# Two chunks of query projections moved from the projection phase into the first segment of the attention

## The chip, the cores and the metric

The kernel runs on one core of one Trainium2 chip. The metric is the device time of one execution in microseconds; the time before is the median of three runs. Tables and quotations from the profile come from one profiled execution of the same kernel.

## The reference: what is computed

Two attention branches work on the same input `x` (2048 positions, width 512, 32 heads of 16):

```
A:  q,k,v = x @ wqkv;  p = softmax(q k^T / 4) over all 2048 keys;  a = (p v) @ wo
B:  q,k,v = x @ wq, wk, wv;  4 segments of 512: causal softmax inside a segment,
    plus a memory of earlier segments (phi(q) M / phi(q) z), mixed by sigmoid(beta);  b = (...) @ wo
out = g a + (1 - g) b,   g = sigmoid(sum(x * gate_w))
```

Only branch A's queries are touched here: `q = x @ wqkv[:, 0:512]`, for 2048 positions in four chunks of 512.

## The kernel before, in words

All products that need full precision are made of two halves: a float32 tile is split into a rounded part (`h`) and its remainder (`l`), and three matmuls, h·l, l·h and h·h, stand for one.

**Projections (lines 277 to 588).** A chunk of 512 positions of `xT` is loaded, split and multiplied. `qk_tile` (line 358) makes one tile: 128 output columns (8 heads, ordered by dimension) by 512 positions, in 4 x 3 = 12 matmuls of 128x512 on line 313. One tile fills one *slot* (`slot`, line 306); other work is posted to a slot and one of four places in it. ScalarE copies the tile out (lines 368, 369), VectorE makes its remainder (line 376), and SP's queue stores both parts in DRAM scratch (`qd`, `kd`; lines 370, 377). Phase A (lines 472 to 484) takes each of the four chunks through 4 tiles of Q, 4 of K and 4 of V: 12 slots a chunk. The next chunk's load and split, and at the last chunk those of branch B's weights, are posted by slot numbers counted from `s0`, the chunk's first slot. Phase B (lines 552 to 587) does the same for branch B, and runs the first 96 maxima of the attention beside it.

**Attention (lines 591 to 985).** A *unit* is a side (A or B), a group of four heads and one segment of 512 queries: `(side, g, c)`. Units stand in the order A0 B0 A1 B1 ... of segment 1 (c = 0), then segment 2, and so on; each A unit has 64 slots, each B unit 10 (592 slots a segment, 2368 in all). A slot is one 128x512 tile of scores. The main loop (line 944) goes through the slots n in an order written out by hand, engine by engine:

- `score_part` (line 662): TensorE makes a score tile (`st`, line 677), ScalarE exponentiates it (line 700). For B, GpSimd masks the diagonal (line 681).
- `max_part` (line 218), 96 slots ahead: TensorE makes the same scores the other way round (`sm`, line 204) in one of four PSUM banks, and VectorE reduces them to maxima (`TENSOR_REDUCE`, line 225; for B a masked minimum, line 237). The maxima become extra rows of the query tile, so that the exponentials of line 700 need no further subtraction.
- every third slot a turn of TensorE: either `some_values` (line 712), which multiplies finished exponentials with V into the bank `ops` (line 733), or, if the list `shared` holds anything, four matmuls of that list in its place.
- when a unit's values are complete, ScalarE copies `ops` out (`oraw`, line 737) and a store follows. An *octet* (line 766) then normalizes eight heads in steps posted by slot with `at(n, f)`: loads, a power on GpSimd (line 792), products and splits on GpSimd.

**Output products.** With the end of each unit of A of segments 2 to 4, `shared` receives 12 matmuls of 128x512 (`output`, line 860; the matmuls are on line 838) that multiply results of the segment before with the output weights. They accumulate in `ops`, and ScalarE copies the bank out (lines 878, 882). Segment 1 has none. The output weights are loaded and split into halves by `load_wo` (line 611), in segment 1: eight loads at slots 30 to 114, 12 apart, each split by GpSimd 8 slots later (lines 623, 624).

SP issues nearly all transfers in the order in which the code gives them, and an issue that waits holds up those behind it. Loads of query and key tiles are issued 20 slots before their first maximum (`PRE`).

Of the kernel before, what the change touches and what calls it, by code (L numbers as in the profile page):

```python
# [10 lines left out]
F32 = mybir.dt.float32  # L11
F32R = mybir.dt.float32r
# [7 lines left out]
D = 512  # L20
H = 32
DH = 16
CH = 512
NCH = S // CH
KT = D // 128
NG = 8
NO = 4
# [6 lines left out]
NU = 32  # L34
LEAD = 96
BURST = 3
MOST = 3
LOW, HIGH = 6, 14
NP = 6
# [7 lines left out]
def gated_mix(ctx, tc, x, xT, wqkv, a_wo, b_wq, b_wk, b_wv, b_wo, beta, gate_w, out):  # L47
    nc = tc.nc
# [5 lines left out]
    qd = {}  # L54
# [59 lines left out]
    for k in range(NU):  # L114
# [3 lines left out]
        start, apart = (33, (3, 3)) if k == 1 else (6, (9, 3)) if k < NU - 1 else (23, (3, 3))  # L118
# [17 lines left out]
    def raw(t):  # L136

        return t[:].bitcast(F32)
# [137 lines left out]
    with ExitStack() as p0:  # L276
# [23 lines left out]
        now = [0]  # L300
# [20 lines left out]
        def halves(pool, tag, src, load_slot, split_slot, tiles=None):  # L321

            hold = {}

            def load(i):
                t = tiles[i] if tiles else None
                if t is None:
                    t = raws.tile([128, 2, D], F32, tag="raw", name="raw")
                if isinstance(t, list):
                    for k in range(2):  # L330
                        nc.sync.dma_start(t[k], src[256 * i + 128 * k:256 * i + 128 * k + 128])
                        hold["raw", 2 * i + k] = t[k]
# [78 lines left out]
        wraw = [raws.tile([128, KT, 256], F32, tag="raw", name="raw")]  # L411
# [58 lines left out]
                post(4 + b // 2, 1 + 2 * (b % 2), lambda b=b: gate_logit(xg[b // 2], b % 2, 4 * c + b))  # L470

        for c in range(NCH):
            s0 = 12 * c
            xn = halves(xp, "x", xchunk((c + 1) % NCH), s0 + (5 if c == 0 else 4), s0 + 8)
            if c == NCH - 1:
                wBq = halves(wp, "wq", b_wq, s0 + 7, s0 + 10)
                wBv = halves(wp, "wk", b_wv, s0 + 9, s0 + 13)
                wBk = halves(wp, "wv", b_wk, s0 + 11, s0 + 15)
            for o in range(NO):
                qk_tile("A", wAq, xc, o, qd["A", o, c])  # L480
            for o in range(NO):
                qk_tile("A", wAk, xc, o, kd["A", o, c])
            v_tiles("A", wAv, xc, c)
            xc = xn
# [67 lines left out]
        s0 = now[0]  # L552
# [46 lines left out]
    wo = ctx.enter_context(tc.tile_pool(name="wo", bufs=1, reuse_waits="tile"))  # L599
    fr = ctx.enter_context(tc.tile_pool(name="fr", bufs=1, reuse_waits="tile"))  # L600
# [5 lines left out]

    ops = o_ps.tile([128, CH], F32, name="ops")

    wos = {}

    def load_wo(side, w, o, n):

        k = {}

        def load():
            if o == 0:
                wos[side] = wo.tile([128, NO, 2, D], F32R, name=f"wo{side}")
            k["t"] = fr.tile([128, D], F32, tag="v", name="woraw", bufs=2)
            nc.sync.dma_start(k["t"], w[128 * o:128 * o + 128])

        def split():
            h = wos[side][:, o]
            nc.gpsimd.tensor_copy(h[:, 0], k["t"])
            nc.gpsimd.tensor_sub(h[:, 1], k["t"], h[:, 0].bitcast(F32))
        at(n, load)
        at(n + 8, split)

    vt = {}

# [82 lines left out]
    def some_values(n, most):  # L712

        while queue and most and queue[0][0] <= n:
            _, u, i = queue.pop(0)
            most -= 1
            side, g, c = u
            w = 1
            while (queue and most and queue[0][0] <= n and queue[0][1] == u and (i + w) // 4 == i // 4
                   and (side == "A" or PIECES[i + w][0] == PIECES[i][0])):  # L720
                queue.pop(0)
                most -= 1
                w += 1
            p = pt_[u, i // 4]
            if side == "A":
                c0 = q0 = 128 * (i % 4)
                v = vt[u][:, i // 16, i // 4 % 4]
            else:
                b, c0, q0 = PIECES[i]
                v = vt[u][:, b]  # L730
            done = i + w == SLOTS[side]
            for h in range(4):
                nc.tensor.matmul(ops[32 * h:32 * h + 17, q0:q0 + 128 * w], v[:, 17 * h:17 * h + 17], p[:, h, c0:c0 + 128 * w],  # L733
                                 start=(i == 0), stop=done, tile_position=(0, 32 * h))
            if done:
                raw = ob.tile([128, CH], F32, tag="o", name="oraw")
                nc.scalar.copy(raw, ops)
                nc.sync.dma_start(od[side, c][4 * g:4 * g + 4].rearrange("h r t -> (h r) t"), raw)
                stored.add(u)
                if side == "B" and c and g % 2 == 0:  # L740
                    octet("M", g // 2, c, n + 4)
                if (side, g ^ 1, c) in stored and u != ("A", NG - 1, NCH - 1):
                    octet(side, g // 2, c, n + (20 if side == "B" and (g < 5 or c < last) else 8))
                if u in between:
                    shared.extend(output(*between[u]))
                return


# [14 lines left out]
    def at(n, f):  # L763
        beside.setdefault(n, []).append(f)
# [69 lines left out]

    def products(ps, t, b, side, o, start, stop):

        for i, (x, w) in enumerate(((1, 0), (0, 1), (0, 0))):
            yield lambda i=i, x=x, w=w: nc.tensor.matmul(ps, t[:, b, x], wos[side][:, o, w], start=start and i == 0,  # L838
                                                         stop=stop and i == 2)

    def out_rows(c, b):
# [3 lines left out]
    shared = []  # L845
# [14 lines left out]
    def output(c, b, pairs, then, ps=ops):  # L860

        ks = [(os, o, i) for os in pairs for o in os for i in range(2)]
        for k in ks:
            def f(n, k=k):
                os, o, i = k
                assert loaded_blocks[c, b, os] > len(blocks) - 2
                t = blocks[loaded_blocks[c, b, os] - 1][:, i, o % 2].unsqueeze(1)
                list(products(ps, t, 0, "AB"[i], o, k == ks[0], k == ks[-1]))[n]()
                if k == ks[-1] and n == 2:
                    then(ps, c, b)  # L870
            for n in range(3):
                yield lambda n=n, f=f: f(n)

    part = {}
# [58 lines left out]
    def most():  # L933
# [44 lines left out]
    for b in range(4):  # L978
# [3 lines left out]
        t = fr.tile([128, D], F32, tag="v" if b % 2 else "res", name="res", bufs=2)  # L982
# [37 lines left out]
```

## Time and profile before

| | before |
|---|---|
| median of three runs | 1807.16 us (1805.61 to 1807.22) |
| the profiled execution, whole | 1806.01 us |
| its span | 1804.1 us |
| PE / PEld busy in the span | 1791.4 / 954.9 us |
| VectorE (DVE) busy | 1571.3 us |
| ScalarE (ACT) busy | 1449.2 us |
| GpSimd (POOL) busy | 604.0 us |

PE is TensorE's matmuls, PEld its loading of weights, SP the queue that issues transfers. A line of a group reads: line of the code, engine, operation, tile written <- tiles read, shapes and count, then busy time and mean ns of one, then the idle time ahead of it and what ended that. A line of a timeline begins with start and length in us. A matmul's end is modelled, and matmuls overlap, so that PE can be shown busy where it isn't at its peak.

### The profile page before, as it was taken

The numbers are of one execution on the slowest core, as the hardware profiler recorded it, in microseconds if no ns is written. First come the engines' busy times: TensorE is split into PE (matmuls) and PEld (weight loads), VectorE is DVE, ScalarE is ACT, GpSimd is POOL, SyncE is SP. The second block draws the span as 40 slices with busy tenths as digits, with TensorE's granted clock in tenths as the row PEclk, the third lists the DMA queues.
The fourth block names the chain that finished last, engine by engine and source line by source line (L and its number), as shares of the span: only waits on it lengthen the run. The fifth ranks groups of instructions, "written<-read, shape, count | busy, mean of one in ns | idle before, by whom it ended". The sixth has DMA issues, their size and how long they took to land.

```text
span 1804.1 us, 42457 instructions
## 1 busy us (share of the span) xinstructions
PE 1791.4 (99%) x15857; PEld 954.9 (53%) x15857; DVE 1571.3 (87%) x3333; ACT 1449.2 (80%) x2766; POOL 604.0 (33%) x708
## 2 busy tenths in 40 slices
PE   9999999999999999999999999999999999999998
PEld 7887766544444544444444444444444444444444
DVE  4224677899999999999999999999999999999920
ACT  5445444788888888888888888888888888888894
POOL 3001222234141414243432534342534342525442
PEclk9999999999999999999999999999999999999999
DMA  7568645543344344545454445454445454444541
GB/s 225 199 220 268 219 166 177 168 125 110 120 109 120 110 119 121 143 127 144 126 144 126 126 141 145 120 142 124 139 124 143 125 145 116 143 130 130 147 146 61
DMA packets 140620, 258.51 MB, mean 143 GB/s; under 512 B 36184, under 2 KB 60280, under 8 KB 139904
## 3 DMA queue, kind: packets, MB, share of 16 engines
q1 hardware_dynamic: 138912, 254.15, 48.3%
q8 instruction: 126, 2.06, 0.5%
q0 software_dynamic: 1216, 1.14, 0.3%
q14 instruction: 78, 0.64, 0.1%
q10 hardware_dynamic: 288, 0.52, 0.1%
HBM read 171.25 MB, written 83.25 MB: 141 GB/s over the span
## 4 chain that ended last, share of the span: by engine, by line
PE 91%; DVE 2%; ACT 2%; DMA 2%; POOL 1%; issue 1%; SPq 0%; POOLq 0%; ACTq 0%; DVEq 0%
PE ops L733 32%; PE st L677 27%; PE sm L204 14%; PE pr L313 10%; PE ops L838 4%; PE sm L838 2%; DVE pm L225 1%; ACT p L700 1%; POOL mn L373 1%; DMA raw<-xT 1%; PE num L495 1%; DMA qdA<-q 0%; DMA vs<-wqkv 0%; DMA qdB<-q 0%; DVE q L376 0%
## 5 line engine op out<-in xcount | busy, mean ns | idle before, releaser
L700 ACT ACTIVATE p<-st 128x512 f32<-128x512 f32 x2261 | 1190.5, 600 | 149.1 <-PE sm L204 95.1
L225 DVE TENSOR_REDUCE pm<-sm 128x1 f32<-128x512 f32 x2048 | 1277.1, 680 | 12.5 <-PE sm L204 11.6
L204 PE MATMUL sm<-kA,qA 48*128 48x512 f32 x2048 | 672.9, 435 | 0.9 <-DVE pm L237 0.7
L677 PE MATMUL st<-qA,kA 50*128 50x512 f32 x2014 | 666.8, 432 | 0.3 <-ACT p L700 0.3
L733 PE MATMUL ops<-p,vA 128*17 128x128 f32 (+3 forms) x7368 | 559.7, 407 | 0.0
L677 PEld LDWEIGHTS st<-qA,kA 50*128 50x128 f32 x2014 | 327.5, 185 | 384.9 <-ACT p L700 337.1
L204 PEld LDWEIGHTS sm<-kA,qA 48*128 48x128 f32 x2048 | 327.6, 184 | 23.4 <-issue 6.7
L792 POOL TENSOR_TENSOR rcp<-rec,minus 128x32 f32<-128x32 f32 x43 | 234.3, 5449 | 118.2 <-DMA rec<-dend 83.0
L733 PEld LDWEIGHTS ops<-p,vA 128*17 128x17 f32 x7368 | 152.3, 96 | 223.7 <-issue 179.5
L237 DVE CUSTOM_DVE_ANT_0 rest<-sm,mask 128x128 f32<-128x128 f32 (+3 forms) x512 | 245.2, 479 | 2.2 <-PE sm L204 1.5
L681 POOL TENSOR_SCALAR_AFFINE_SELECT p<-p 128x512 f32<-128x512 f32 x128 | 79.5, 640 | 349.5 <-ACT p L700 346.7
L204 PE MATMUL sm<-kB,qB 48*128 48x128 f32 (+3 forms) x512 | 166.1, 384 | 0.0
L376 DVE TENSOR_TENSOR q<-full,q 128x512 fp32r<-128x512 f32 x64 | 44.4, 694 | 86.5 <-ACT q L369 84.9
L677 PE MATMUL st<-qB,kB 50*128 50x512 f32 (+1 forms) x495 | 115.7, 333 | 1.8 <-ACT p L700 1.5
L677 PEld LDWEIGHTS st<-qB,kB 50*128 50x128 f32 x495 | 72.5, 186 | 59.2 <-ACT p L700 50.9
L733 PE MATMUL ops<-p,vB 128*17 128x128 f32 (+3 forms) x1480 | 88.1, 353 | 0.1
L204 PEld LDWEIGHTS sm<-kB,qB 48*128 48x128 f32 x512 | 79.9, 184 | 0.0
L368 ACT COPY full<-pr 128x512 f32<-128x512 f32 x64 | 37.4, 584 | 50.4 <-PE pr L313 50.2
L373 POOL TENSOR_SCALAR mn<-full 128x512 f32<-128x512 f32 x24 | 35.7, 1489 | 101.7 <-ACT full L368 81.3
L186 POOL CAST ms<-pm 128x16 fp32r<-128x16 f32 x32 | 6.3, 198 | 174.7 <-DVE pm L237 174.7
L186 POOL CAST ms<-nm 128x16 fp32r<-128x16 f32 x32 | 6.7, 210 | 169.7 <-DVE nm L182 169.7
L313 PE MATMUL pr<-xh,wql 128*128 128x512 f32 x128 | 54.7, 427 | 0.1
(178 smaller groups left out, 1590.6 us busy)
## 6 DMA issues: line engine op xcount, KB each, us to landing
kA<-kdA SPq DMA_DIRECT2D x256, 128.0 KB
vA<-vdA SPq DMA_DIRECT2D x31, 544.0 KB
kA<-kdA SPq DMA_DIRECT2D x256, 64.0 KB
qdA<-q SPq DMA_DIRECT2D x32, 256.0 KB
kdA<-q SPq DMA_DIRECT2D x32, 256.0 KB
qdB<-q SPq DMA_DIRECT2D x32, 256.0 KB
qA<-qdA SPq DMA_DIRECT2D x64, 128.0 KB
kdB<-q SPq DMA_DIRECT2D x32, 256.0 KB
```

Of the source, the lines that this page charges most:

```text
L204: nc.tensor.matmul(ps[:, n0:n0 + n], rows(qt[u][:, :, s * 128:(s + 1) * 128], h, 48), rows(k[:, :, k0:k0 + n], h, 48), start=True, stop=True)
L225: nc.vector.tensor_reduce(pm[:, h, s, kc:kc + 1], ps, axis=AX.X, op=ALU.max)
L237: rows_left.append(lambda h=h, s=s, n0=n0, w=w: nc.vector.tensor_tensor_reduce(out=tri["rest"][:, 0:w], in0=ps[:, n0:n0 + w], in1=tri["mas ...
L313: nc.tensor.matmul(ps, l(a, k), r(b, k), start=(n == 0), stop=(n == 11))
L373: nc.gpsimd.tensor_scalar_min(ph["mn"], full, 0.0)
L376: nc.vector.tensor_sub(q2, full, q1.bitcast(F32))
L677: nc.tensor.matmul(ps[:, n0:n0 + CH - q0], rows(k[:, :, b * 128:(b + 1) * 128], h, 50), rows(q[:, :, q0:], h, 50), start=True, stop=True)
L681: nc.gpsimd.affine_select(out=x, in_=x, pattern=[[0, 4], [1, 128]], base=0, channel_multiplier=-1, compare_op=ALU.is_ge, fill=0.0)
L700: nc.scalar.activation(p[:, h], ps, AF.Exp, scale=SCALE)
L733: nc.tensor.matmul(ops[32 * h:32 * h + 17, q0:q0 + 128 * w], v[:, 17 * h:17 * h + 17], p[:, h, c0:c0 + 128 * w], start=(i == 0), stop=done ...
L792: eng.tensor_tensor(r, rec, minus, op=ALU.pow)
L838: yield lambda i=i, x=x, w=w: nc.tensor.matmul(ps, t[:, b, x], wos[side][:, o, w], start=start and i == 0, stop=stop and i == 2)
```

## The change: what it does

Phase A leaves out the four Q tiles of chunks 3 and 4 (`LATER = (2, 3)`), so that these chunks have 8 slots in place of 12. `s0` is set back by 4 for them, so that what is posted keeps its distance to the end of the chunk.

The eight tiles are made in the attention's first segment instead. At the end of each unit of A with c = 0, `shared` receives a new list, `later_tile`: the 12 matmuls of one tile, from halves of W_q and of the chunk of `xT` that are loaded and split again (by GpSimd this time). After the twelfth, ScalarE copies the tile out, GpSimd splits it, and two stores write it to `qd` 12 slots later. The units behind A0 to A3 make chunk 3, those behind A4 to A7 chunk 4.

The halves lie in the two tiles that later hold the output weights. W_q and chunk 3 are loaded at slots 2, 10, ... 58; chunk 4 takes the place of chunk 3 after the fourth tile; the output weights are loaded after the eighth, from its end at steps of 8 slots. The raw loads now go through the tiles tagged `res` instead of `v`.

```diff
+LATER = (2, 3)
...
-            s0 = 12 * c
+            s0 = now[0] - (4 if c in LATER else 0)
...
-            for o in range(NO):
+            for o in range(NO if c not in LATER else 0):
                 qk_tile("A", wAq, xc, o, qd["A", o, c])
...
-    def load_wo(side, w, o, n):
+    def load_halves(key, tag, src, o, n):
...
-                wos[side] = wo.tile([128, NO, 2, D], F32R, name=f"wo{side}")
-            k["t"] = fr.tile([128, D], F32, tag="v", name="woraw", bufs=2)
+                halved[key] = wo.tile([128, NO, 2, D], F32R, tag=tag, name="w" + tag)
+            k["t"] = fr.tile([128, D], F32, tag="res", name="wraw", bufs=2)
...
+    def load_pair(a, b, n):
+
+        for o in range(NO):
+            for i, (key, tag, src) in enumerate((a, b)):
+                load_halves(key, tag, src, o, n + 8 * (2 * o + i))
+
+    def later_tile(c, o):
+
+        def done():
+            full = fr.tile([128, CH], F32, tag="part", name="full")
+            nc.scalar.copy(full, ops)
+            t = fr.tile([128, 2, 2, 2, 128], F32R, tag="blk", name="qhalves", bufs=2)
+            t = t.rearrange("p a o h t -> p a (o h t)")
+            nc.gpsimd.tensor_copy(t[:, 0], full)
+            nc.gpsimd.tensor_sub(t[:, 1], full, t[:, 0].bitcast(F32))
+            for i in range(2):
+                at(n + 12, lambda i=i: nc.sync.dma_start(
+                    qd["A", o, c][16 * i:16 * i + 16].rearrange("d h t -> (d h) t"), raw(t[:, i])))
+            if o == NO - 1 and c == LATER[0]:
+                for k in range(KT):
+                    load_halves(("x", LATER[1]), "B", xT[:, LATER[1] * CH:(LATER[1] + 1) * CH], k, n + 2 + 8 * k)
+            elif o == NO - 1:
+                load_pair(("A", "A", a_wo), ("B", "B", b_wo), n + 2)
+
+        def f(i):
+            k, (a, b) = i // 3, ((1, 0), (0, 1), (0, 0))[i % 3]
+            nc.tensor.matmul(ops, halved["q"][:, k, a, o * 128:(o + 1) * 128], halved["x", c][:, k, b],
+                             start=(i == 0), stop=(i == 11))
+            if i == 11:
+                done()
+        for i in range(12):
+            yield lambda i=i: f(i)
...
                 if u in between:
                     shared.extend(output(*between[u]))
+                if side == "A" and c == 0:
+                    shared.extend(later_tile(LATER[g // NO], g % NO))
...
-    for i, (side, w) in enumerate((("A", a_wo), ("B", b_wo))):
-        for o in range(NO):
-            load_wo(side, w, o, 30 + 12 * (4 * i + o))
+    load_pair(("q", "A", wqkv[:, 0:D]), (("x", LATER[0]), "B", xT[:, LATER[0] * CH:(LATER[0] + 1) * CH]), 2)
```

More of the change, by code (lines that the diff above doesn't have):

```diff
@@ L607, in gated_mix @@
     ops = o_ps.tile([128, CH], F32, name="ops")
-    wos = {}
-    def load_wo(side, w, o, n):
+    halved = {}
+    ready = set()
+    def load_halves(key, tag, src, o, n):
         k = {}
@@ L616, in load @@
             if o == 0:
-                wos[side] = wo.tile([128, NO, 2, D], F32R, name=f"wo{side}")
-            k["t"] = fr.tile([128, D], F32, tag="v", name="woraw", bufs=2)
-            nc.sync.dma_start(k["t"], w[128 * o:128 * o + 128])
+                halved[key] = wo.tile([128, NO, 2, D], F32R, tag=tag, name="w" + tag)
+            k["t"] = fr.tile([128, D], F32, tag="res", name="wraw", bufs=2)
+            nc.sync.dma_start(k["t"], src[128 * o:128 * o + 128])
         def split():
-            h = wos[side][:, o]
+            h = halved[key][:, o]
             nc.gpsimd.tensor_copy(h[:, 0], k["t"])
             nc.gpsimd.tensor_sub(h[:, 1], k["t"], h[:, 0].bitcast(F32))
+            ready.add((key, o))
         at(n, load)
         at(n + 8, split)
+    def load_pair(a, b, n):
[20 more added lines that the diff above has]
+            k, (a, b) = i // 3, ((1, 0), (0, 1), (0, 0))[i % 3]
+            assert {("q", k), (("x", c), k)} <= ready
+            nc.tensor.matmul(ops, halved["q"][:, k, a, o * 128:(o + 1) * 128], halved["x", c][:, k, b],
[4 more added lines that the diff above has]
+            yield lambda i=i: f(i)
     vt = {}
@@ L835, in products @@
     def products(ps, t, b, side, o, start, stop):
+        assert (side, o) in ready
         for i, (x, w) in enumerate(((1, 0), (0, 1), (0, 0))):
-            yield lambda i=i, x=x, w=w: nc.tensor.matmul(ps, t[:, b, x], wos[side][:, o, w], start=start and i == 0,
+            yield lambda i=i, x=x, w=w: nc.tensor.matmul(ps, t[:, b, x], halved[side][:, o, w], start=start and i == 0,
                                                          stop=stop and i == 2)
```

## The prediction

> **What bounds the kernel now.** I read the page from the top: busy times, slices, then the chain of the work that ended last.
>
> ```profile
> PE 1791.4 (99%) x15857; PEld 954.9 (53%) x15857; DVE 1571.3 (87%) x3333; ACT 1449.2 (80%) x2766; POOL 604.0 (33%) x708
> ...
> DVE  4224677899999999999999999999999999999920
> ...
> PEclk9999999999999999999999999999999999999999
> ...
> PE 91%; DVE 2%; ACT 2%; DMA 2%; POOL 1%; issue 1%; SPq 0%; POOLq 0%; ACTq 0%; DVEq 0%
> ```
>
> TensorE looks like the bound throughout: 99% busy, 91% of the chain. But VectorE goes from 2 to 4 tenths in the first slices to 9 in all slices of the attention, so there are two regimes, and the page's PE row can't tell which engine holds the second one. The view of busy time by window can. I cut it at ends of units of A, the copies `oraw` on line 737: A0 of segment 1 (372.76), A0 of segment 2 (731.76), A0 of segment 3 (1097.45) and A0 of segment 4 (1461.71). Each stretch holds the same 8 pairs of units (8 x 64 slots of A, 8 x 10 of B). Two stretches of the projections stand ahead: chunks 3 and 4 of A, from one first tile's copy to the next. Columns: length, then busy time (instructions) of PE, PEld, DVE, ACT, POOL, then clock, DMA share, GB/s.
>
> ```profile
> 79.61:112.25 32.64, 32.64 (x145) 27.04 (x144) 8.04 (x12) 14.10 (x24) 0.33 (x1) 1.00 0.58 195
> 112.25:144.89 32.64, 32.64 (x145) 27.04 (x144) 11.50 (x17) 16.80 (x29) 0.44 (x2) 1.00 0.80 263
> ...
> 372.76:731.76 359.00, 356.80 (x3644) 173.32 (x3643) 359.00 (x776) 318.46 (x616) 110.19 (x140) 1.00 0.41 118
> 731.76:1097.45 365.69, 365.69 (x3635) 175.66 (x3636) 364.47 (x780) 324.42 (x626) 144.45 (x164) 1.00 0.50 134
> 1097.45:1461.71 364.26, 364.26 (x3636) 174.59 (x3636) 363.03 (x776) 322.92 (x624) 144.91 (x164) 1.00 0.49 134
> ```
>
> In segment 1 VectorE is busy 359.00 of 359.00 us: not one gap. Its groups there, and in segment 3 (the third of these stretches), which has exactly as many instructions of each kind:
>
> ```profile
> L225 DVE TENSOR_REDUCE pm<-sm 128x1 f32<-128x512 f32 x512 | 317.3, 676 | 0.0
> L237 DVE CUSTOM_DVE_ANT_0 rest<-sm,mask 128x128 f32<-128x128 f32 (+3 forms) x128 | 60.8, 475 | 0.0
> ...
> L225 DVE TENSOR_REDUCE pm<-sm 128x1 f32<-128x512 f32 x512 | 319.6, 681 | 0.4
> L237 DVE CUSTOM_DVE_ANT_0 rest<-sm,mask 128x128 f32<-128x128 f32 (+3 forms) x128 | 61.5, 480 | 0.8 <-PE sm L204 0.7
> ```
>
> So the attention's first segment is bound by VectorE's 640 maxima, and TensorE only has to deliver scores in time. The projections are the other regime: PE 32.64 of 32.64, VectorE 8.04 or 11.50, ScalarE 14.10 or 16.80.
>
> TensorE's 99% needs weighing here, since on it hangs whether anything more fits beside VectorE. In segment 1 PE is busy 356.80 of 359.00, weight loads (PEld) 173.32, or 48%. [...] Segments 2 and 3, which carry an extra load of TensorE, decide it with their own lengths.
>
> **The change, part by part.**
>
> *Removed: 8 tiles from the projections.* Loop `for o in range(NO)` over Q of A is empty for two chunks; a tile is 12 matmuls in one slot. Slots of chunk 4:
>
> ```profile
> 112.25 0.59 ACT L368 COPY full<-pr 128x512 f32<-128x512 f32 x1 [2.13 <-PE pr L313]
> 114.97 0.59 ACT L368 COPY full<-pr 128x512 f32<-128x512 f32 x1 [1.48 <-PE pr L313]
> ...
> 144.89 0.59 ACT L368 COPY full<-pr 128x512 f32<-128x512 f32 x1 [1.61 <-PE pr L313]
> ```
>
> From 112.25 to 144.89 are 12 slots in 32.64 us: 2.72 us each, first and last alike, without a stall. Chunk 3 has the same 32.64. Gone: 8 x 2.72 = **-21.76 us**. The two copies, one subtraction and two stores a tile that go with them lay beside TensorE and were worth nothing. Loads and splits of x and of B's weights keep their distance to the end of each chunk (`s0` is set 4 back), so they are as early as before, counted from their use.
>
> *Added: the same 96 matmuls in segment 1*, four in each of three turns in place of the values' matmuls, behind each of 8 units of A. Segment 1 has no such turns before; segments 2 to 4 have, with output products of the same count and shape: 12 of 128x512 behind each unit, accumulated in the same bank `ops`, which ScalarE then copies out.
>
> ```profile
> 824.63 0.96 PE L838 MATMUL ops<-woA,blk 128*128 128x512 f32 x3
> ...
> 825.75 0.38 PE L677 MATMUL st<-qB,kB 50*128 50x256 f32 x1
> ...
> 826.70 0.73 PE L838 MATMUL ops<-woB,blk 128*128 128x512 f32 x2
> ...
> 827.83 0.50 PE L677 MATMUL st<-qA,kA 50*128 50x512 f32 x1
> ...
> 828.78 0.51 PE L838 MATMUL ops<-woA,blk 128*128 128x512 f32 x1
> ...
> 829.91 0.50 PE L677 MATMUL st<-qA,kA 50*128 50x512 f32 x1
> ```
>
> These are the three turns of one unit: 1.12 + 1.13 + 1.13 = 3.38 us from the first product to the next score. What of it reaches VectorE is the difference of equal segments: 364.26 - 359.00 = **+5.26 us** (776 VectorE instructions in both), 0.66 a unit. Segment 2 says the same: 6.69 longer with 780 instructions; four more of them (two reductions and one masked minimum with its read-out at the cut) are some 1.8, leaving 4.9. That is an average over all that segments 2 and 3 have more than segment 1, so I take 5.26. Bounds: 0 (all hidden) and 10.5 (twice that, if the queue of values, not yet settled behind A0, drains worse).
>
> *Added on ScalarE:* 8 copies of 128x512, of which segments 2 and 3 also have 8 (lines 878, 882): in the 5.26.
>
> *GpSimd.* Before, 8 loads of output weights are split in segment 1; after, 12 loads of W_q and x and 8 results, and the output weights only at its end.
>
> ```profile
> L623 POOL CAST woB<-woraw x4: 611/612/614, 378.6 to 402.9; 128x512 fp32r<-128x512 f32 x4
> L624 POOL TENSOR_TENSOR woB<-woraw,woB x4: 1280/1287/1291, 379.3 to 403.6; 128x512 fp32r<-128x512 f32 x4
> L792 POOL TENSOR_TENSOR rcp<-rec,minus 128x32 f32<-128x32 f32 x8 | 43.6, 5450 | 4.3 <-DMA rec<-odA 4.3
> ```
>
> A split is 0.61 + 1.29 = 1.90 us. In the whole kernel there are 20 more (12 loads, 8 results), 38 us, covered by GpSimd's idle time, 359.00 - 110.19 in segment 1; with all of it there GpSimd is as busy as in segments 2 and 3 (144 us). Behind a split wait the masks of B's diagonals; they already stand behind 5.45 us powers. If that cover fails, B's values come a split late, 1.9 us, at a unit: I take 0 and keep 2.
>
> *The first tile* needs 8 loads (n = 2 to 58) split by slot 66, and reads the last pair in its third turn, some 8 slots (5 us) later. Loads of this kind made GpSimd wait:
>
> ```profile
> 367.64 0.61 POOL L623 CAST woA<-woraw 128x512 fp32r<-128x512 f32 x1 [7.72 <-DMA woraw<-a_wo]
> ```
>
> That split began when its load had landed, 7.72 us after GpSimd was free. As much on the last pair would cost TensorE up to 7.7 - 5 = 3 us, once: taken as 0, kept for the range.
>
> *SP's queue* gets 12 loads and, in place of 16 stores in the projections, 16 in segment 1, each behind a wait for GpSimd. Behind them stand the loads of keys, issued 20 slots (12 us, at 359.00 / 592 = 0.61 a slot) ahead.
>
> ```profile
> SPq L738 <- ACT oraw L737: 69.1, 16, 6.9
> SPq L201 <- ACT mt L198: 45.4, 4, 12.3
> ...
> SPq L801 <- POOL rec L798: 15.7, 4, 5.0
> ```
>
> SP already waits up to 12.3 us in this segment, and VectorE has no gap. Cost 0; the two new waits of a store come 12 slots (7 us) after its split is asked for.
>
> *The projections' transfers.* A Q tile is two stores.
>
> ```profile
> qdA<-q SPq DMA_DIRECT2D x32, 256.0 KB
> ```
>
> Chunk 4 moves 263 GB/s x 32.64 us = 8.6 MB; without four Q tiles of 0.52 MB it is 6.5 MB in 21.76 us, 298 GB/s. The busiest quarter before has 296 at a share of 0.92:
>
> ```profile
> 128.57:136.73 8.16, 8.16 (x37) 6.76 (x36) 4.57 (x7) 5.71 (x10) 0.00 (x0) 1.00 0.92 296
> 144.89:187.70 42.81, 42.29 (x207) 34.49 (x206) 21.94 (x43) 26.31 (x45) 8.31 (x7) 1.00 0.80 261
> ```
>
> It is tight, yet TensorE was full in that quarter. If only the 263 of the whole chunk could be had, 6.5 MB would take 24.7 us: 2.9 late. I take 0.
>
> *Sum:* the profiled execution took 1806.01 us (span 1804.1 and 1.9 around it). 1806.01 - 21.76 + 5.26 = 1789.5. The median of three runs, 1807.16, is 1.15 above it; on that basis **1790.7 us**, -0.9%.
>
> **The rivals.**
>
> *All hidden.* TensorE's room swallows the turns, and the 5.26 belongs to other work that segments 2 and 3 have more (GpSimd 144 against 110 us, transfers 134 against 118 GB/s). 1807.16 - 21.76 = 1785.4. Against it: the idle time that VectorE shows in segment 3 is nearly all for scores of TensorE (0.7 of 0.8 us ahead of L237).
>
> *Twice the price or a late piece*: 10.5 instead of 5.26, or the 2 to 3 us of a late split, load or weight on top: 1793 to 1798. For it: the chunk at 298 GB/s and the first tile's deadline.
>
> *Slower: TensorE is the bound in the attention too*, as chain and busy row say. Then each tile costs its three turns in full, 8 x 3.38 = 27.0 us against 21.76 saved: 1812.4. Its place is a turn of four products at the end of a unit of A; it decides from the point at which the four score banks don't carry VectorE (four reductions, 2.47 us below) over a turn of 1.13 us. Against it: segments 2 and 3 pay 0.66 of 3.38 a unit.
>
> *Slower by GpSimd holding VectorE up:* 38 us more of splits, each blocking VectorE: 1790.7 + 38 = 1829.
>
> ```profile
> 489.71 2.47 DVE L225 TENSOR_REDUCE pm<-sm 128x1 f32<-128x512 f32 x4
> ...
> 512.38 5.47 POOL L792 TENSOR_TENSOR rcp<-rec,minus 128x32 f32<-128x32 f32 x1 [1.00 <-DMA rec<-odA]
> ...
> 513.09 4.27 DVE L225 TENSOR_REDUCE pm<-sm 128x1 f32<-128x512 f32 x7
> ```
>
> Seven reductions beside a power of GpSimd take 4.27 us, four beside an idle GpSimd 2.47: 0.60 for each further one in both. [...]
>
> *The change doesn't do what it says*, if slots of the projections were paced by transfers: the gain would shrink by the 2.9 above. The even 2.72 speaks against it; it lies in the second rival.
>
> **How the numbers follow.** Forecast 0.64, all hidden 0.12, twice or late 0.18, slower by TensorE 0.04, by GpSimd 0.02. The range takes in the first three with their bounds: 1785.4 to 1798; 0.06 lies outside by mechanism, and I leave the rest for sizes. A measurement here tells about 0.2% (3.6 us) from no change. Faster 0.93; within 0.2% (the late pieces all together, or a third of the slower rival) 0.02; slower 0.05.
>
> **What would show it.** Right: chunks 3 and 4 take 21.76 us each; the attention begins some 21.8 us earlier; segment 1, from A0's end, takes 364 us with VectorE still over 99% busy and gaps only behind units of A; segments 2 to 4 keep their lengths. Wrong: gaps between `pr` matmuls near the end of chunk 4 (transfers); a segment 1 of 386 us (TensorE); reductions with a mean well over 681 ns away from unit ends (GpSimd); VectorE waiting for loads of keys (SP).

## The result, and the profile after

The changed kernel takes 1798.23 us, the median of eight runs (1795.30 to 1804.83), and the kernel before 1806.12 us (eight runs, 1805.61 to 1807.22). The ratio is 0.9958 with a 95% interval of 0.9946 to 0.9970. That is 7.9 us faster where 16.5 had been forecast: the sign was right, the gain is half of what the sum gave, and the median lies 0.2 us above the top of the range.

The profiled execution of the changed kernel took 1796.78 us (span 1795.1), 9.2 less than that of before. Its busy row:

```profile
PE 1780.0 (99%) x15729; PEld 938.1 (52%) x15729; DVE 1570.9 (88%) x3325; ACT 1443.9 (80%) x2758; POOL 640.3 (36%) x748
```

GpSimd has 40 instructions and 36 us more, VectorE and ScalarE 8 instructions less, as the change says. The 128 that TensorE has less are products of values, 8720 for 8848: while the tile's turns are taken values collect, and a matmul behind them takes more of them. Where the time went is seen in the view of busy time by window, cut at the same events as in the prediction (columns as there): chunk 3, chunk 4, phase B up to the first exponential of the attention, then segments 1, 2 and 3 from A0's copy to A0's copy (`oraw` is on line 774 now).

```profile
79.39:101.15 21.76, 21.76 (x97) 18.02 (x96) 5.27 (x8) 9.26 (x17) 0.32 (x1) 1.00 0.59 197
101.15:122.91 21.76, 21.76 (x97) 18.02 (x96) 8.73 (x13) 11.95 (x22) 0.44 (x2) 1.00 0.90 298
122.91:307.86 184.95, 183.47 (x862) 131.54 (x860) 127.08 (x240) 91.00 (x156) 45.13 (x44) 1.00 0.62 207
350.43:721.44 371.01, 366.80 (x3612) 174.22 (x3611) 363.55 (x776) 322.98 (x625) 132.59 (x164) 0.99 0.45 127
721.44:1088.47 367.03, 366.08 (x3635) 175.81 (x3636) 364.98 (x780) 324.34 (x627) 149.62 (x170) 1.00 0.49 138
1088.47:1453.05 364.58, 364.58 (x3636) 174.73 (x3636) 363.04 (x776) 322.92 (x624) 144.64 (x164) 1.00 0.48 134
```

The two chunks give back 32.64 - 21.76 = 10.88 us each, 21.76 together, with PE busy 21.76 of 21.76. A0 of segment 1 ends at 350.43 in place of 372.76, 22.33 earlier. Segment 1 then takes 371.01 in place of 359.00: 12.01 us more, where 5.26 was the term of the sum. Segment 2 takes 1.34 more, segment 3 0.32. So 22.33 - 12.01 - 1.34 - 0.32 = 8.66 us are left at A0 of segment 4, and 9.0 at the end.

Segment 1 is eight pairs of units. Seven of them are 0.55 to 0.73 us longer than before (mean 0.63). The pair from A3's copy to A4's holds all the rest. It is shown here after, then before:

```profile
487.02:540.11 53.09, 48.88 (x449) 22.84 (x449) 46.53 (x99) 40.93 (x80) 29.21 (x33) 0.94 0.48 137
```

```profile
507.44:552.94 45.50, 45.25 (x460) 22.22 (x461) 45.50 (x99) 40.38 (x79) 20.08 (x24) 1.00 0.45 125
```

It is 7.59 us longer, and the mean granted clock of TensorE fell to 0.94. The view of waits of the changed kernel in this pair (engine and operation that waited, what ended the wait: us in total, times, longest) has TensorE and VectorE stand still there once each:

```profile
PEld mt_ps L196 <- POOL ms L188: 4.5, 1, 4.5
PE mt_ps L196 <- POOL ms L188: 4.2, 1, 4.2
DVE rest L238 <- PE sm L205: 5.1, 1, 5.1
```

`ms` is made of the finished maxima of a unit: VectorE reduces them to `nm` (line 183), GpSimd splits `nm` into two halves `ms` (lines 187, 188), TensorE transposes `ms` into `mt_ps` (line 196), and the result becomes the extra rows of the query tile. The transposes are posted 9 slots behind the unit's last maximum (`LATE_T`), in TensorE's own order. If `ms` isn't there, scores for exponentials and for maxima stand behind the transpose, and VectorE runs dry. Here it is the maxima of A5. VectorE's and GpSimd's timelines after:

```profile
517.11 0.20 DVE L183 TENSOR_REDUCE nm<-pm 128x16 f32<-128x64 f32 x1
```

```profile
495.86 5.46 POOL L831 TENSOR_TENSOR rcp<-rec,minus 128x32 f32<-128x32 f32 x1
...
507.37 0.22 POOL L188 TENSOR_TENSOR ms<-pm,ms 128x16 fp32r<-128x16 f32 x1
508.33 0.61 POOL L625 CAST wB<-wraw 128x512 fp32r<-128x512 f32 x1 [0.74 <-DMA wraw<-xT]
...
514.41 0.61 POOL L625 CAST wB<-wraw 128x512 fp32r<-128x512 f32 x1 [4.10 <-DMA wraw<-xT]
515.10 1.29 POOL L626 TENSOR_TENSOR wB<-wraw,wB 128x512 fp32r<-128x512 f32 x1
518.68 5.43 POOL L831 TENSOR_TENSOR rcp<-rec,minus 128x32 f32<-128x32 f32 x1 [2.29 <-DMA rec<-odB]
...
525.83 0.20 POOL L187 CAST ms<-nm 128x16 fp32r<-128x16 f32 x1
526.11 0.22 POOL L188 TENSOR_TENSOR ms<-nm,ms 128x16 fp32r<-128x16 f32 x1
```

VectorE's `nm`, GpSimd's split and TensorE's transposes of the same maxima before:

```profile
537.07 0.20 DVE L182 TENSOR_REDUCE nm<-pm 128x16 f32<-128x64 f32 x1
```

```profile
527.50 5.43 POOL L792 TENSOR_TENSOR rcp<-rec,minus 128x32 f32<-128x32 f32 x1
...
537.34 0.20 POOL L186 CAST ms<-nm 128x16 fp32r<-128x16 f32 x1 [2.61 <-DVE nm L182]
537.61 0.22 POOL L187 TENSOR_TENSOR ms<-nm,ms 128x16 fp32r<-128x16 f32 x1
```

```profile
541.60 0.39 PE L195 MATMUL mt_ps<-identf,ms 128*32 128x128 f32 x4
```

Before, GpSimd waited 2.61 us for the maxima, `ms` was done at 537.83, and the transposes came at 541.60: a margin of 3.8 us. After, `nm` is done at 517.31 and `ms` at 526.33, 9.0 us later in place of 0.56, because GpSimd, which works its queue off in order, has the octet's power (5.43 us) and its followers ahead of it. Before, that power began 9.6 us ahead of `nm`; now it begins 1.6 us behind it. Three things hold it back. Behind the halves of B's maxima (507.37), where the power followed at once before, GpSimd now splits x twice, and waits for both loads (0.74 and 4.10 us). The power's own load `rec<-odB` comes late (2.29). And the octet itself is posted later: the code counts its steps from the slot in which the values of B3 are complete, and the tile's turns go ahead of those values. SP's issue of that load, before and then after:

```profile
520.91 0.63 SPq L778 DMA_DIRECT2D rec<-odB  x1
```

```profile
515.69 0.62 SPq L817 DMA_DIRECT2D rec<-odB  x1
```

That is 13.5 us into the pair before and 28.7 after, where it now stands behind the loads of B's next query and key tiles. SP, which issues it, waits for GpSimd too:

```profile
SPq L621 <- POOL wB L626: 3.8, 2, 3.5
```

SP's loads of x need a raw buffer, and the two raw buffers come free with a split of GpSimd: engine and queue hold each other up.

The wait is 4.2 to 4.5 us, and the pair lost 7. The rest is TensorE's clock, seen in TensorE's timeline and in windows after the wait:

```profile
520.60 0.39 PE L205 MATMUL sm<-kA,qA 48*128 48x512 f32 x1
...
526.38 0.64 PE L196 MATMUL mt_ps<-identf,ms 128*32 128x128 f32 x2 [4.21 <-POOL ms L188]
...
528.08 0.62 PE L205 MATMUL sm<-kA,qA 48*128 48x512 f32 x1
```

```profile
527.00:529.00 2.00, 2.00 (x12) 1.13 (x15) 0.95 (x4) 1.48 (x4) 1.86 (x3) 0.50 0.02 4
533.00:535.00 2.00, 2.00 (x19) 0.77 (x17) 1.76 (x3) 1.57 (x3) 0.00 (x0) 1.00 0.51 150
```

The granted clock is 0.50 behind the wait, the same score matmul takes 0.62 us in place of 0.39, and VectorE is busy 0.95 of 2 us. From 525.4 to 532.2 the clock is 0.50 and on both sides of that 1.00: 6.8 us of half clock.

### The profile page after: what moved, and what is told of

Its sections match the earlier page's. It is cut to its first block, busy times and chain, and to the rows that moved or that the text cites. A ratio compares the mean times of both kernels' runs of the same rounds, so it can differ in the third digit from the quotient of the medians.

```text
span 1795.1 us, 42234 instructions
## 1 busy us (share of the span) xinstructions
PE 1780.0 (99%) x15729; PEld 938.1 (52%) x15729; DVE 1570.9 (88%) x3325; ACT 1443.9 (80%) x2758; POOL 640.3 (36%) x748
## 4 chain that ended last, share of the span: by engine, by line
PE 90%; DMA 2%; ACT 2%; POOL 2%; DVE 1%; issue 1%; SPq 1%; POOLq 0%; ACTq 0%; DVEq 0%
PE ops L770 32%; PE st L714 26%; PE sm L205 14%; PE pr L314 9%; PE ops L878 4%; PE sm L878 2%; PE ops L658 2%; ACT p L737 1%; POOL mn L374 1%; DMA raw<-xT 1%; POOL rcp L831 1%; PE num L496 1%; DMA vs<-wqkv 1%; DMA qdB<-q 0%; PE mt_ps L196 0%
## 5 line engine op out<-in xcount | busy, mean ns | idle before, releaser
L205 PE MATMUL sm<-kA,qA 48*128 48x512 f32 x2048 | 662.9, 431 | 0.1
L770 PE MATMUL ops<-p,vA 128*17 128x256 f32 (+3 forms) x7216 | 557.4, 412 | 0.0
L377 DVE TENSOR_TENSOR q<-full,q 128x512 fp32r<-128x512 f32 x56 | 38.8, 693 | 71.3 <-ACT q L370 71.3
L369 ACT COPY full<-pr 128x512 f32<-128x512 f32 x56 | 32.6, 582 | 38.8 <-PE pr L314 38.4
```

Source lines behind the costliest of these rows:

```text
L205: nc.tensor.matmul(ps[:, n0:n0 + n], rows(qt[u][:, :, s * 128:(s + 1) * 128], h, 48), rows(k[:, :, k0:k0 + n], h, 48), start=True, stop=True)
L377: nc.vector.tensor_sub(q2, full, q1.bitcast(F32))
```

## The experiments

My theory from these rows was: the lost 7 us are one event, the transposes of A5's maxima waiting for GpSimd, and its causes are the late x loads and splits in GpSimd's and SP's queues. The rivals: the tile's matmuls cost that much in this pair (TensorE or transfers), or the work taken out of the projections has to be paid elsewhere. Where no run of the kernel before is given, it ran beside at 1806.6 to 1808.2 us. The changed kernel has only the runs above, so that the experiments are compared with it through their ratios to the kernel before. Each pair is one profiled execution.

**The part removed alone** (kernel before, without the eight tiles, with `s0` set back as in the change; queries of chunks 3 and 4 are read from 1 and 2).

```diff
-            for o in range(NO):
+            for o in range(NO if c < 2 else 0):
                 qk_tile("A", wAq, xc, o, qd["A", o, c])
...
-        src = qd[side, g // 2, c]
+        src = qd[side, g // 2, c % 2 if side == "A" else c]
```

> The removal alone: the kernel before without the 8 Q tiles; the queries of chunks 3 and 4 are read from those of chunks 1 and 2 (that part of the computation is changed), and nothing is added to the attention. The first copy of the attention came 22.3 us earlier in the changed kernel: by that 1806.1 - 22.3 = 1783.8. By the prediction's own term 21.76: 1784.4. If part of the loss sits in the projections after all (transfers): above 1786.

1785.47 us, ratio 0.9877 (0.9861 to 0.9894), 22.7 less. Its segment 1:

```profile
350.37:710.60 360.23, 358.07 (x3644) 173.67 (x3643) 359.37 (x776) 318.40 (x617) 110.25 (x140) 1.00 0.42 118
```

The removal is worth its full 21.76, and segment 1 without the added work is 1.2 us longer at most. All of that lies in its first pair, in which score matmuls took 0.62 us in place of 0.40 for a time (see the end). What the change lost, it lost by the added part.

**The transposes later, first try.** The transposes of one unit are posted 10 slots later.

```diff
                 due = min(e for e in a_last if e >= last_max[u]) + LATE_T
+                if u == ("A", 4, 0):
+                    due += 10
```

> The transposes of the maxima of one unit, A4 of segment 1, are asked for 10 slots (6 us) later; nothing else changes. Theory Q (GpSimd's queue delivers these maxima 9.0 us after VectorE, TensorE waits 4.5 us for them in order and then runs at half clock for 6.8 us): the pair A3 to A4 falls from 53.1 to about 45.6 us, TensorE's granted clock stays at 1.00, the time is 1790 to 1791 and its runs lie closer together. Rival T (transfers and SP's queue are late in this stretch, and the transpose is only where it shows): the same delay turns up at the next thing that waits, the pair stays above 50 us and the time at 1797 to 1799.

1796.6 us, ratio 0.9938 (0.9921 to 0.9954). The pair from A3 to A4 still had its wait, and was still long:

```profile
PE mt_ps L196 <- POOL ms L188: 3.6, 1, 3.6
```

```profile
487.15:538.60 51.45, 47.81 (x449) 22.36 (x449) 46.50 (x99) 40.88 (x80) 29.30 (x33) 0.97 0.51 141
```

I had named the wrong unit: what is late in this pair are A5's maxima, made 96 slots ahead, not A4's. As it stands the run is a control: a later request for a unit whose maxima are in time leaves the stall where it was.

**The transposes later, the right unit**: the same edit with `("A", 5, 0)`.

> As the first experiment meant it, with the right unit: the transpose of the maxima of A5 (the one that the trace shows late) is asked for 10 slots (6 us) later; GpSimd and all transfers keep their order. Theory Q (TensorE waits in order for maxima that GpSimd delivers 9.0 us after VectorE): no wait is left, the pair A3 to A4 takes 45.6 to 46.2 us, no half clock in it; 0.991 of before (about 1790). Rival T (transfers and SP are late as such): the pair stays above 50 us, 0.995 of before.

1790.42 us, ratio 0.9914 (0.9901 to 0.9928). The pair:

```profile
488.36:534.64 46.28, 46.28 (x449) 22.27 (x449) 46.22 (x99) 41.14 (x81) 29.23 (x33) 1.00 0.55 151
```

`ms` still comes 8.3 us behind `nm`, the loads and splits keep their order, and only TensorE no longer asks for it in that time. The pair is 0.78 longer than before, close to the 0.55 to 0.73 of the seven others, and the clock stays at 1.00. This run shows the cause: the wait of TensorE, and neither the tile's matmuls nor its transfers.

**The loads of x for chunk 4 later**, from 2 slots after the tile to 26.

```diff
-                    load_halves(("x", LATER[1]), ..., k, n + 2 + 8 * k)
+                    load_halves(("x", LATER[1]), ..., k, n + 26 + 8 * k)
```

> The four loads of x for chunk 4 start 24 slots later, so that their splits stand behind the power of B's octet and the maxima of A4 in GpSimd's queue. Same amount of work and of bytes. Theory Q: the maxima are no longer late, the pair A3 to A4 takes about 45.6 us, the time is 1790 to 1791. Rival T': it is the amount of extra work of GpSimd and of transfers in segment 1 that costs, wherever it stands: 1797 to 1799, the loss moves to another unit.

1792.77 us, ratio 0.9915 (0.9900 to 0.9930). The pair, and its wait:

```profile
488.89:536.05 47.16, 46.45 (x448) 22.06 (x449) 46.07 (x99) 40.89 (x80) 29.07 (x33) 1.00 0.57 149
```

```profile
PE mt_ps L196 <- POOL ms L188: 0.7, 1, 0.7
```

`ms` is 5.5 us behind `nm`, a little more than the margin, and 0.7 us of wait is left. The clock doesn't fall. The ratio is level with that of A5's later transposes (0.9914).

**No second x** (chunk 4's loads left out; its tiles are made from chunk 3's halves, so these queries are not the reference's).

```diff
-            if o == NO - 1 and c == LATER[0]:
-                for k in range(KT):
-                    load_halves(("x", LATER[1]), ...)
...
-            nc.tensor.matmul(ops, ..., halved["x", c][:, k, b],
+            nc.tensor.matmul(ops, ..., halved["x", LATER[0]][:, k, b],
```

> The four loads and splits of x for chunk 4 are left out, and its four tiles are computed from the halves of chunk 3 (that part of the computation is changed). All 96 matmuls stay. Theory Q: without these splits the maxima come in time; the pair A3 to A4 takes about 45.6 us; 1789.5 to 1790.5. Rival U (the price of the matmuls of one tile is itself uneven, and this tile costs 7.6 us): the pair stays at 53 us and the time at 1797 to 1799.

1793.38 us, ratio 0.9921 (0.9906 to 0.9936). The pair from A3 to A4, and the first pair of segment 2 in the same execution:

```profile
489.36:535.47 46.11, 46.11 (x448) 21.92 (x449) 46.04 (x99) 40.90 (x80) 21.82 (x25) 1.00 0.49 135
716.87:768.17 51.30, 49.13 (x469) 23.50 (x471) 46.20 (x100) 41.08 (x79) 20.91 (x25) 0.93 0.50 145
```

The stall of segment 1 is gone. `ms` is 3.4 us behind `nm` here (0.56 before). The tile's turns do that to the octet by themselves: the power has no split of x ahead of it and waits 5.43 us for `rec<-odB`. TensorE doesn't wait for `ms`. The other 5.7 us of the lateness come with the loads and splits of x. But this execution, the longest of its four, had another stall at the start of segment 2. There TensorE waited for masks of B0 that stood behind the splits of the output weights, and the clock fell here as well (0.93 in the pair):

```profile
PE ops L766 <- POOL p L714: 2.2, 1, 2.2
```

It is the same kind of event in another place, 5.2 us in this execution and 0.9 in the profiled one of the changed kernel. That its size depends on when loads land, and that the spread of the changed kernel (9.5 us between its eight runs, 1.6 in the kernel before beside it, 5.1 in 16 later runs of that) is such events coming and going, is argued from this; its longest run was not profiled.

**Four raw buffers of their own** in place of two shared ones, so that SP doesn't wait for splits.

```diff
-            k["t"] = fr.tile([128, D], F32, tag="res", name="wraw", bufs=2)
+            k["t"] = fr.tile([128, D], F32, tag="wraw", name="wraw", bufs=4)
```

> Four raw buffers of their own for the added loads in place of the two shared ones, so that SP's queue never waits for a split before it issues such a load. GpSimd's work and order are unchanged. Theory Q as GpSimd's work alone: little changes, the pair A3 to A4 stays at 50 us or above. Theory Q-SP (the maxima are late because the loads ahead of them in GpSimd's queue, and the octet's, were issued late by SP, which waited 3.8 us for GpSimd): the pair falls to 46 to 48 us.

1793.5 us, ratio 0.9934 (0.9920 to 0.9947):

```profile
489.01:537.64 48.63, 46.48 (x448) 22.04 (x449) 46.09 (x99) 40.89 (x81) 29.18 (x33) 1.00 0.55 149
```

```profile
PE mt_ps L196 <- POOL ms L188: 2.2, 1, 2.2
```

`ms` comes 7.0 us behind `nm` in place of 9.0. So SP's wait for splits is 2 us of the lateness, and without it the wait is 2.2 us and the clock doesn't fall. The pair lies between what the two theories gave. GpSimd still waits here, 2.03 us for a load of x and 3.13 for `rec<-odB`: the rest is the order of loads and splits, and the octet's later place in it.

**Buffers and later transposes together** (the last edit and the one for A5).

> The changed kernel with two edits: four raw buffers for the added loads, and the transpose of A5's maxima 10 slots later. By the sum of the two single runs: the pair A3 to A4 at 46.2, the first pair of segment 2 within 0.5 us of before, 1788.5 to 1790 or 0.990 to 0.991 of before. If the two cures are the same one (SP's wait): no better than the late transpose alone, 0.9914.

1790.92 us, ratio 0.9912 (0.9898 to 0.9925), not to be told from the transposes alone: with nobody waiting for `ms`, an earlier `ms` is worth nothing. The pairs came as expected, 46.27 from A3 to A4 and 46.24 at the start of segment 2, where the later transposes alone have 47.77; the time was 0.9 us above the expected range. In the profiled executions that first pair of segment 2 takes 46.20 to 46.24 us with four raw buffers (46.14 before) and 46.55 to 51.30 with two.

**The wait without the half clock.** Twenty idle matmuls of 128x512 stand ahead of the transposes of A5's maxima, so that TensorE is busy while it would wait.

```diff
+        if us[-1][1] == ("A", 5, 0):
+            for _ in range(20):
+                nc.tensor.matmul(pt, halved["q"][:, 0, 0, 0:128], halved["q"][:, 0, 0], start=True, stop=True)
```

> The changed kernel with 20 idle matmuls of 128x512 (4.5 us) ahead of the two transposes for which TensorE waits behind A3, so that it works in place of waiting. The maxima are as late as before. Theory Q with the clock as a second price (4.5 us of waiting, then 6.8 us at half clock that cost some 3 us more): the wait stays, as work, but the clock stays at 1.00; the pair A3 to A4 takes 50 to 50.5 us in place of 53.1. If the clock had no part: 53 us.

1795.69 us, ratio 0.9942 (0.9929 to 0.9956). The pair, and the idle matmuls:

```profile
488.64:539.63 50.99, 50.99 (x468) 25.53 (x469) 46.09 (x99) 40.89 (x80) 29.25 (x33) 1.00 0.53 143
```

```profile
523.56 4.84 PE L197 MATMUL mt_ps<-wA 128*128 128x512 f32 x20
```

TensorE loses 4.84 us for the scores as it did in the wait, but the clock stays at 1.00. From the pair without a wait (46.28) it is 4.7 us to this one, and 2.1 more to the changed kernel's (53.09). So the event is about 4.7 us of standing still and 2.1 us of half clock, by one execution of each.

**Both sets of loads moved**: x for chunk 4 from 34 slots at steps of 6, the output weights at steps of 6 in place of 8.

```diff
-                    load_halves(("x", LATER[1]), ..., k, n + 2 + 8 * k)
+                    load_halves(("x", LATER[1]), ..., k, n + 34 + 6 * k)
...
-                load_pair(("A", "A", a_wo), ("B", "B", b_wo), n + 2)
+                load_pair(("A", "A", a_wo), ("B", "B", b_wo), n + 2, 6)
```

> The changed kernel with the splits for chunk 4 behind A5's maxima in GpSimd's queue (loads 32 slots later, 6 apart) and those of the output weights 6 slots apart, so that the last stands ahead of B's diagonals of segment 2. Same work. Theory Q: no wait of TensorE for GpSimd is left, segment 1 takes 364 us as predicted, the first pair of segment 2 46.1 to 46.5, no half clock; by the prediction's own terms 1806.1 - 22.3 + 5.3 = 1789, ratio 0.9905, and the runs within 3 us. If the extra GpSimd work or traffic costs wherever it stands: 0.993 or more.

1797.04 us, ratio 0.9949 (0.9935 to 0.9963): a miss. The pair from A3 to A4 was 46.10 as expected; the last pair, A7 to A0, was 51.61:

```profile
671.06:722.67 51.61, 47.05 (x449) 21.41 (x447) 45.46 (x97) 39.57 (x78) 36.30 (x40) 0.94 0.65 171
```

Its waits, TensorE's and SP's, and SP's timeline:

```profile
PE st L714 <- DMA qB<-mt: 4.6, 1, 4.6
```

```profile
SPq L621 <- POOL wB L626: 5.5, 1, 5.5
```

```profile
713.98 0.34 SPq L621 DMA_DIRECT2D wraw<-b_wo  x1
714.42 1.41 SPq L202 DMA_DIRECT2D qB<-mt  x2
```

The steps of 6 slots are too short for two raw buffers. A load of an output weight waited 5.5 us on SP for a split, the store of B0's extra rows stood behind it, and TensorE waited 4.6 us for that store.

**The same with four raw buffers.**

> The last kernel again (splits for chunk 4 behind A5's maxima, output weights 6 slots apart) with four raw buffers of their own. Theory: the loss of the last run, 7.7 us ahead of segment 2, came because SP's queue waited up to 5.5 us for a split before it could issue a load, and the store of B0's maxima stood behind that load. With four buffers SP doesn't wait: all pairs of segment 1 at 44.5 to 46.3, segment 1 in 364 to 365 us, no half clock; 1788.5 to 1790.5, ratio 0.990 to 0.991. If the extra GpSimd work itself were the cause: again a pair above 50 us, 0.994.

1789.93 us, ratio 0.9908 (0.9895 to 0.9922). Segments 1 and 2:

```profile
351.56:715.91 364.35, 364.35 (x3612) 173.41 (x3611) 363.15 (x776) 322.84 (x624) 135.94 (x167) 1.00 0.48 131
715.91:1081.66 365.75, 365.75 (x3635) 175.53 (x3636) 364.37 (x780) 324.26 (x626) 146.55 (x167) 1.00 0.51 136
```

TensorE's matmuls have no wait over 0.3 us left in the attention, segment 1 takes the 364 us that the prediction gave it (364.35 against 359.00: 5.35 for eight tiles), and the time is within 1 us of the forecast. By its median it is the fastest of the kernels here that compute all of the reference, 16.7 us below the kernel before (1806.59), but its interval overlaps with those of the two with later transposes for A5 and of the later loads of x.

**The queue alone, without the change.** In the kernel before, five idle splits (0.61 + 1.29 us each) go to GpSimd at slot 336, just ahead of the end of A5's maxima, and in a second run at slot 342, just behind it.

```diff
+    dum = fr.tile([128, 2, CH], F32R, name="dum")
+
+    def more():
+        for _ in range(5):
+            nc.gpsimd.tensor_copy(dum[:, 0], tri["mask"])
+            nc.gpsimd.tensor_sub(dum[:, 1], tri["mask"], dum[:, 0].bitcast(F32))
+    at(336, more)
```

> The kernel before with five idle splits (9.5 us of GpSimd, no transfer, result unused) put into GpSimd's queue at slot 336, just ahead of A5's maxima; nothing else of the change. Theory Q: the maxima come some 7.5 us late, TensorE waits about 3 us for them, and the pair A3 to A4 goes from 45.5 to 48.5 us, or to 50 to 52 if the wait is long enough for the half clock; the time rises by 3 to 7 us. Rival (the loss needs the change's transfers or its matmuls): no change from before.

> The control: the same five idle splits in the kernel before, six slots later, just behind A5's maxima in GpSimd's queue. Theory Q: within 0.1% of before, pair A3 to A4 at 45.5 us, since what follows there has the time. If 9.5 us of GpSimd work in this stretch cost by themselves: as the run above.

Ahead of the maxima: 1812.15 us, ratio 1.0031 (1.0019 to 1.0043), 5.6 us slower. The pair and TensorE's wait:

```profile
507.74:559.19 51.45, 47.96 (x461) 23.15 (x461) 46.08 (x99) 40.42 (x79) 29.30 (x34) 0.93 0.42 111
```

```profile
545.52 0.64 PE L195 MATMUL mt_ps<-identf,ms 128*32 128x128 f32 x2 [3.25 <-POOL ms L187]
```

Behind them: 1807.06 us, ratio 1.0002 (0.9993 to 1.0011), and the pair as before:

```profile
509.47:554.98 45.51, 45.26 (x460) 22.26 (x461) 45.51 (x99) 40.39 (x80) 29.45 (x34) 1.00 0.45 125
```

GpSimd is as busy in the one (29.30) as in the other (29.45). The same 9.5 us of work cost 6 us of the pair in one place of the queue and nothing a few slots on.

## Why the prediction was half right

**The removed tiles: right.** 21.76 forecast, 21.76 measured in the chunks; A0 of segment 1 ends 22.33 earlier, and 20.0 to 22.4 in the profiled executions of all kernels without these tiles.

**The price of a tile in segment 1: right.** 0.66 a unit forecast from the difference of segments 3 and 1; 0.63 measured in the seven pairs without a stall, and 5.35 for all eight in the kernel without waits. Segments 2 and 3, with the same matmuls in them, were the right price list. TensorE is not the bound there, which answers the slower rival: seven pairs would have been 3.4 us longer each. So the busy row (PE 356.80 of 359.00 us in segment 1 before) didn't show what room TensorE had, and the lengths of segments 2 and 3 did. Whether the share of weight loads (48%) measures that room, no run tests. One sign was not as foreseen: of the 5.35 us, 4.15 are VectorE's own busy time (363.15 against 359.00 for the same 776 instructions) and only 1.2 are gaps. What makes its instructions longer, no run separates.

**The projections' transfers: right at 0.** Chunk 4 ran at 298 GB/s and a DMA share of 0.90, with PE full.

**ScalarE's copies, and the loads of the first tile: right at 0.** The first pair is 0.56 longer than before, like the others. GpSimd holding VectorE up didn't show either: with the idle splits behind the maxima GpSimd is busy 29.45 us in the pair in place of 20.08, and the pair and VectorE's work in it take 45.51 as against 45.50.

**GpSimd: wrong, and this is the step that failed.** The prediction set the splits against "GpSimd's idle time, 359.00 - 110.19", and took 0 and kept 2 for "B's values come a split late, 1.9 us, at a unit". Idle time in sum says nothing about one result that is due 3.8 us later. I looked at one consumer behind the splits, the masks, and not at the other, the maxima's halves on which TensorE's transposes wait. Nor did I add the queue up: it was not one split of 1.9 us but a split that itself waits for its load, and behind that a power of 5.4 us whose load is late. Nor did I see that the tile's turns push B's octet back. The margin could be read in the trace of before: from the end of `ms` to the first `mt_ps` 3.0 to 4.4 us in segment 1, less than one power, and down to 0.8 us in segments 2 to 4, where output products take the same turns. These segments were the price list for the matmuls, and had no splits of x beside them. The two runs with idle splits show that work in GpSimd's queue is enough for such an event, if it stands ahead of the result.

**SP's queue: wrong at "Cost 0".** I counted the transfers that stand behind the new stores, and found them early enough. I didn't count that a new load waits for its raw buffer, that is for GpSimd, and that octet loads stand behind it. Without this wait (own buffers) the lateness of `ms` falls by 2.0 us, the wait from 4.2 to 2.2, and the profiled stall from 7.6 to 3.1. The 0.9 us at the start of segment 2 fell to 0.1 in that run as well.

**No term for TensorE's clock.** A wait of 4 us was thinkable in the "late piece" rival, but priced at itself, 2 to 3 us. It cost 4.7 and 2.1 on top.

The rival "twice the price or a late piece" (1793 to 1798) is the one that came true, as a late piece: 1789.5 + 7 for the one pair and 1 for segment 2 is 1797.5 on the profiled execution's basis, where 1796.78 was measured. It came true in kind, not in size: its late piece was priced at 2 to 3 us, and its top of 1798 needs twice the price of the turns as well, which was not paid. That the time lies so close to that top is luck. The median of the eight runs is 1.45 us above the profiled one, and what that holds is not known.

## What to carry to other kernels

Added work on GpSimd, which works off its queue in order, was priced here by what stands behind it in the queue: the same 9.5 us of splits cost 6 us of the pair ahead of the maxima and nothing behind them. For each result, the time between its end and its consumer's turn is the room there is (3.8 us for A5's maxima before), and the engine's idle time in sum (359.00 - 110.19 us) is not. Where an added load takes a buffer that another engine frees, its queue is a second such place (a load waited 5.5 us on SP for a split, and TensorE 4.6 us for the store behind it), and both are to be followed to the engine that sets the end. Steps whose slot is counted from work that the change delays move too (3.4 us between `nm` and `ms` in place of 0.56, with no second x loaded). Put the added work just behind the results with a small margin, or ask for those results later: ten slots for one unit were worth 7.8 us here.

## What the runs showed of the hardware

TensorE's granted clock fell at waits of 3.25 us (idle splits ahead of the maxima, 0.93 on the mean of the pair), 4.2 (the changed kernel, 0.94) and 4.6 (both sets of loads moved, 0.94), and less at one of 3.6 (the transposes later, first try, 0.97). In the changed kernel it was 0.50 for 6.8 us; behind the waits of 3.25 and 4.6 us score matmuls take 0.62 us as they do there. It didn't fall at a wait of 0.7 us (the loads of x later, 1.00 in the pair) nor at one of 1.4 (the transposes later for A5, 1.000 over the execution). At 2.2 us both are seen: it stayed at 1.00 in the run with own buffers, and fell in the run without a second x (0.93 in the pair), where the score matmuls behind the wait take 0.62 us again:

```profile
728.33 1.05 PE L766 MATMUL ops<-p,vB 128*17 128x256 f32 x8 [2.17 <-POOL p L714]
...
730.34 0.62 PE L205 MATMUL sm<-kA,qA 48*128 48x512 f32 x1
```

So the length of the wait alone doesn't decide.

One thing stays open. Matmuls were as slow in two places without such a wait. In the run with the part removed alone score matmuls took 0.63 and 0.62 us at 354.60 and 355.14, and 0.40 again at 357.31. In the run with the idle splits behind the maxima they took 0.62 us at 377.10 and 377.64, and the mean clock was 0.93 in this stretch of it, from A0's copy to A1's:

```profile
372.23:420.10 47.87, 47.39 (x457) 22.77 (x455) 45.67 (x98) 40.47 (x80) 12.86 (x19) 0.93 0.36 107
```

It took 47.87 us where the kernel before takes 45.32, and TensorE had no wait there over 0.48 us. The first score matmuls of 0.79 us in place of 0.50 began 3.6 us behind the copy of A0 of segment 1 in the one (354.01) and 2.1 us in the other (374.37). The kernel before seems to have such spells too: of its 32 runs beside the experiments, 14 have a mean granted clock of 1.000 and a median of 1805.2 us, and 18 a lower clock (0.997 to 0.999) and 1807.8 us; none of the 18 was profiled. Neither a trace nor a run here tells what brings them on.
